# Two more output pairs by seven products, with the attention work visited inside them, in a retention and bilinear-FFN kernel on one Trainium2 core

## Chip, cores and metric

The kernel runs on one core of one Trainium2 chip. The metric is the device time of one execution in microseconds (us), the median of several runs. Engines are named as in the profile: PE (matrix products), DVE (VectorE), ACT (ScalarE), POOL (GpSimd), SP (it issues the transfers).

## The reference

A linear recurrent attention (retention) over 4 batches, 8 heads, 768 steps and 64 columns a head, whose output feeds a bilinear feed-forward layer over 3072 tokens:

```python
for t in range(S):
    state = gamma[None, :, None, None] * state + np.einsum('bhd,bhe->bhde', k[:, :, t], v[:, :, t])
    y[:, :, t] = scale * np.einsum('bhd,bhde->bhe', q[:, :, t], state)
...
x = np.ascontiguousarray(attn_out.transpose(0, 2, 1, 3)).reshape(B * S, H * D)
a = x @ w_a
b = x @ w_b
return (a * b @ w_out).astype(np.float32)
```

Inputs and output are float32. w_a and w_b are 512 x 1536, w_out is 1536 x 512.

## The kernel before

**Slots and tiles.** A slot is 128 tokens of one batch with all heads; there are 24. `TILES` groups them into eight tiles J of 4, 2, 2, 2, 2, 4, 4, 4 slots. J=0 holds slots 0 to 3, J=1 slots 4 and 5, J=2 slots 6 and 7, J=3 slots 8 and 9. The first six slots (three pairs) go through a chunked attention of their own (`casts2`, `flip2`, `scores2` and so on); the later ones go through `casts`, `turn` and `leave`.

**Attention of the later slots.** `casts(t)` scales k and q of slot t by decay tables into bf16 (`scaled`, POOL), has SP transpose them by DMA into `kqT`, casts v into `vb` (POOL), and after an odd slot has SP load the next two (`load_slot`: one transfer for k, two for q, one for v). `turn(new, old)` is PE's part for two slots at a time: it multiplies the older two with the running states (`inter`), makes the state products (`chunk_states`) and scores (`scores`) of the newer two, and finishes the older (`intra`). The sums of the state products run on DVE at once. Their casts to bf16 (`gst`, ACT) and the copies of a finished pair into the next tile's x (`leave`, ACT) are put into the list `later`, from which `catch_up(n)` takes n; the masking of the scores (DVE) is put into `unmasked`, from which `mask_now(n)` takes n.

**FFN of a tile.** For each of twelve blocks ft of 128 inner columns, `ffn_ab` makes a (4 matmuls, copied to SBUF as `asb` by ACT) and g (4 matmuls), and DVE multiplies g with `asb` into `ht` (line 625). The products' PSUM banks come from the pool `psff` with three banks; for the pairs in `SPARE` (tiles 2 to 4, odd ft) they come from the two banks of `psat` that are named y0 and y1. `parts` divides the matmuls of J=0 from ft 2 on into two halves of columns.

**Outputs.** J=0 and J=1 use `ffn_out`: for each slot 12 matmuls of 512 columns into one bank, which ACT copies out (line 659, 662). The tiles in `FAST` use `ffn_fast`, once for a pair of slots: a 2 x 2 block product by seven half-size products instead of eight, each of six matmuls of 256 columns (`product`, line 784). This needs sums of blocks of `ht` (`add` into `hsum`, four for each tile, line 682) and differences of blocks of w_out (`combine_o` into `wt_bf`, DVE, line 225). Between the products ACT takes snapshots of the banks (`keep`) and DVE adds banks and snapshots into the output (`plus`, line 799). A pair in `ASIDE` has the seventh product in a bank of its own, early; else it is the last one, added into R1.

**What sets the order.** The kernel writes every engine's order by hand: `seq` chains each instruction behind the one before it on its engine. Tile 1's twelve blocks (`blocks(1)`) stand ahead of J=0's outputs. The table `ahead` says what attention work is called at a visit: (J, ft) ahead of a block, (J, "o", i) ahead of output slot i, and "mid", "late" and "sums" inside `ffn_fast`. `adds_of` says after which ft the sums of a tile are made. Slots 8 and up have their k and q waiting in the raw buffers, 3 for each of k, q and v, which hold two slots each.

Of the kernel before, what the change touches and what calls it, by code (L numbers as in the profile page):

```python
# [9 lines left out]
F32 = mybir.dt.float32  # L10
# [17 lines left out]
def kernel(  # L28
# [209 lines left out]
    def scaled(eng, t, i):  # L238
        ktab, qtab = tabs[0] if t < 2 * PAIRS else tabs[1]
        dst, src, tab = kqb[t][:, i], raws["kq"[i], t], (ktab, qtab)[i][:, t % NCH]  # L240
        dst = dst.rearrange("p hp r d -> p r hp d")
        src = src.rearrange("p (r hp) d -> p r hp d", r=2)
        tab = tab.rearrange("p (r hp) o -> p r hp o", r=2).to_broadcast([P, 2, HP, D])
        if t < 10:
            seq(eng.tensor_tensor(dst, src, tab, op=ALU.mult))  # L245
        else:
            for r in range(2):
                seq(eng.tensor_tensor(dst[:, r], src[:, r], tab[:, r], op=ALU.mult))  # L248
# [6 lines left out]
    def casts(t, names="kqv"):  # L255
        if "k" in names:
            new_nat(t)
            scaled(nc.gpsimd, t, 0)
            scaled(nc.gpsimd, t, 1)
            kqT[t] = tra.tile([P, 2, HP, P], BF16, tag="kqT", name="kqT", bufs=6)  # L260
            seq(nc.sync.dma_start_transpose(
                out=kqT[t].rearrange("p a b c -> p (a b) c"),
                in_=kqb[t].rearrange("p a hp r d -> p (a hp r d)")))
# [326 lines left out]
    def parts(J, ft, c0, c1, n):  # L590
# [11 lines left out]
    def ffn_a(J, ft, c0=0, c1=None):  # L602
# [5 lines left out]
        for kt in range(KT):  # L608
            for b0, b1 in parts(J, ft, c0, c1, NFT):
                seq(nc.tensor.matmul(a[:, b0 - c0 : b1 - c0], wa_bf[:, kt, fs], xcols(J, kt, b0, b1),  # L610
                                     start=(kt == 0 and b0 == c0), stop=(kt == KT - 1 and b1 == c1),
                                     skip_group_check=True))
# [3 lines left out]
    def ffn_g(J, ft, c0=0, c1=None):  # L616
# [3 lines left out]
        for kt in range(KT):  # L620
            for b0, b1 in parts(J, ft, c0, c1, NFT):
# [45 lines left out]

    def rows(J, r, par, f0, f1):
        h = ht[J].rearrange("p (f r) (u par m) -> p r f u par m", r=2, par=2, m=P)
        return h[:, r, f0:f1, : TILES[J] // 2, par]  # L670
# [116 lines left out]
    def ffn_fast(J, u):  # L787
# [170 lines left out]
    for j in range(NO):  # L958
# [26 lines left out]
    def adds_of(J, ft):  # L985
        if J == 4:
# [34 lines left out]
    def blocks(J):  # L1021
        done = blocks_seven(J) if J in SEVEN else 0
        for ft in range(done, NFT):
# [3 lines left out]
            ffn_ab(J, ft)  # L1027
            if J in FAST:
# [52 lines left out]
```

## Time and profile before

| | us |
|---|---|
| median of 3 runs | 220.08 (219.37 to 220.78) |
| the profiled execution | 219.07 |
| its span, first to last instruction | 217.4 |
| PE busy in it | 210.2 (97%) |
| DVE busy | 143.5 (66%) |
| POOL busy | 120.1 (55%) |
| ACT busy | 96.9 (45%) |

The granted clock of TensorE was 1.000. A row of a timeline reads: start, duration (us), engine, line, operation, what is written and read, its shape, how many; in brackets the idle time ahead of it, and what ended that. A row of the chain has the same start, with what was on the path to the end. A group has its busy time in all, the mean of one in ns, and the idle time ahead of the group. The stage that the change touches lies between 40 and 70 us: tile 1's blocks from 40.08, the six output slots of J=0 and J=1 from 50.67 to 68.48, and from there on tile 2.

### The profile page before, as it was taken

How to read it: one execution, taken by the hardware profiler on the slowest of the kernel's cores; microseconds unless marked ns; L12 is line 12 of the kernel's file. 1: busy time of each engine (PE TensorE's matmuls, PEld its weight loads, DVE VectorE, ACT ScalarE, POOL GpSimd, SP SyncE). 2: the span in 40 equal slices, each digit the busy share in tenths (PEclk: the TensorE clock that was granted, in tenths of full speed). 3: DMA queues.
4: the chain of work that ended last, by engine and by line, in shares of the span. 5: the costliest groups of instructions: out<-in, count | busy, mean ns of one | idle time of the engine just before them, and what ended most of it. 6: DMA issues, size and time to landing. Idle time of an engine off the chain costs nothing.

```text
span 217.4 us, 7056 instructions
## 1 busy us (share of the span) xinstructions
PE 210.2 (97%) x2871; PEld 155.5 (72%) x2875; DVE 143.5 (66%) x324; ACT 96.9 (45%) x240; POOL 120.1 (55%) x185
## 2 busy tenths in 40 slices
PE   7799999999999999999999999999999999999993
PEld 6578898885446888888878445488665488666682
DVE  2784447647706787698785388987877674777731
ACT  3775244342426436437465342736441642444231
POOL 6557788684554625255462524646989508087400
PEclk9999999999999999999999999999999999999999
DMA  6999999988998998598878969997700002200022
GB/s 176 347 376 382 370 294 368 374 191 157 214 281 190 254 261 188 113 242 189 190 150 191 268 141 249 174 218 129 241 0 3 3 0 100 98 0 5 0 96 97
DMA packets 94832, 39.77 MB, mean 183 GB/s; under 512 B 76112, under 2 KB 91728, under 8 KB 94800
## 3 DMA queue, kind: packets, MB, share of 16 engines
q1 hardware_dynamic: 94656, 39.20, 69.1%
q8 instruction: 22, 0.36, 0.7%
q10 hardware_dynamic: 144, 0.13, 0.2%
q14 instruction: 10, 0.08, 0.1%
HBM read 28.31 MB, written 6.29 MB: 159 GB/s over the span
## 4 chain that ended last, share of the span: by engine, by line
PE 90%; DMA 3%; DVE 2%; POOL 1%; ACT 1%; issue 1%; SPq 0%; POOLq 0%; DVEq 0%
PE g L622 28%; PE a L610 22%; PE o L784 19%; PE o L659 7%; PE a L724 6%; DMA kf<-in_k_dram 3%; PE y L371 2%; PE at L326 1%; POOL kqb L245 1%; PE y L383 1%; PE st L296 1%; DVE ht L625 1%; PE tp L462 1%; PE st L503 1%; DVE aT L487 1%
## 5 line engine op out<-in xcount | busy, mean ns | idle before, releaser
L625 DVE TENSOR_TENSOR ht<-g,asb 128x256 bf16<-128x256 f32 (+1 forms) x98 | 53.8, 549 | 40.2 <-PE g L622 30.4
L622 PE MATMUL g<-xt,wb_bf 128*128 128x256 bf16 (+1 forms) x432 | 77.7, 308 | 0.3 <-ACT asb L614 0.3
L610 PE MATMUL a<-xt,wa_bf 128*128 128x256 bf16 (+1 forms) x368 | 60.9, 296 | 0.1
L614 ACT CAST asb<-a 128x256 bf16<-128x256 f32 (+1 forms) x82 | 36.9, 451 | 51.5 <-PE a L610 51.3
L622 PEld LDWEIGHTS <-wb_bf 128*128 128x128 bf16 x432 | 42.1, 98 | 16.5 <-issue 0.4
L610 PEld LDWEIGHTS <-wa_bf 128*128 128x128 bf16 x368 | 35.3, 98 | 12.3
L248 POOL TENSOR_TENSOR kqb<-kf,ktab 128x256 bf16<-128x256 f32 x28 | 17.2, 635 | 29.5 <-DMA kf<-in_k_dram 21.3
L209 POOL CAST vb<-vf 128x512 bf16<-128x512 f32 x24 | 14.7, 624 | 15.7 <-DMA vf<-in_v_dram 10.4
L784 PEld LDWEIGHTS <-hsum 128*128 128x128 bf16 x216 | 21.0, 98 | 2.7
L796 ACT COPY snap<-o 128x256 f32<-128x256 f32 x34 | 12.7, 375 | 19.6 <-PE o L784 19.4
L784 PE MATMUL o<-wt_bf,hsum 128*128 128x256 bf16 x162 | 19.4, 273 | 0.0
L248 POOL TENSOR_TENSOR kqb<-qf,qtab 128x256 bf16<-128x256 f32 x28 | 16.9, 625 | 3.0 <-DMA qf<-in_q_dram 3.0
L784 PEld LDWEIGHTS <-ht 128*128 128x128 bf16 x162 | 15.4, 98 | 2.5
L659 PE MATMUL o<-wo_bf,ht 128*128 128x512 bf16 x69 | 15.9, 379 | 0.2
L682 POOL TENSOR_TENSOR hsum<-ht 128x256 bf16<-128x256 bf16 (+1 forms) x15 | 11.0, 733 | 9.0 <-DVE ht L625 9.0
L310 DVE TENSOR_TENSOR sums<-st,sums 128x256 f32<-128x256 f32 x30 | 12.7, 423 | 1.5 <-PE st L296 0.2
L784 PE MATMUL o<-wo_bf,ht 128*128 128x256 bf16 x108 | 13.3, 273 | 0.0
L207 ACT CAST gst<-sums 128x256 bf16<-128x256 f32 x33 | 12.5, 412 | 0.5 <-DVE sums L308 0.3
L659 PEld LDWEIGHTS <-ht 128*128 128x128 bf16 x72 | 6.9, 98 | 7.9
L682 DVE TENSOR_TENSOR hsum<-ht 128x256 bf16<-128x256 bf16 (+1 forms) x32 | 12.1, 384 | 0.3
L245 POOL TENSOR_TENSOR kqb<-kf,ktab 128x512 bf16<-128x512 f32 x7 | 7.7, 1100 | 8.0 <-DMA kf<-in_k_dram 8.0
L332 DVE TENSOR_TENSOR aT<-at,mask 128x512 bf16<-128x512 f32 x18 | 12.1, 681 | 0.0
(101 smaller groups left out, 271.7 us busy)
## 6 DMA issues: line engine op xcount, KB each, us to landing
out_dram<-osb SPq DMA_DIRECT2D x11, 512.0 KB, 3.5
kf<-in_k_dram SPq DMA_DIRECT2D x18, 256.0 KB, 4.0
qf<-in_q_dram SPq DMA_DIRECT2D x36, 128.0 KB, 3.7
vf<-in_v_dram SPq DMA_DIRECT2D x18, 256.0 KB, 3.9
wsta<-in_moe_w_a_dram SPq DMA_DIRECT2D x6, 512.0 KB, 7.6
wstb<-in_moe_w_b_dram SPq DMA_DIRECT2D x6, 512.0 KB, 7.8
wsto<-in_moe_w_out_dram SPq DMA_DIRECT2D x6, 512.0 KB, 10.1
kf<-in_k_dram SPq DMA_DIRECT2D x3, 512.0 KB, 6.0
```

The source lines that it names most:

```text
L209: seq(engine.tensor_copy(dst, src))
L248: seq(eng.tensor_tensor(dst[:, r], src[:, r], tab[:, r], op=ALU.mult))
L310: seq(nc.vector.tensor_tensor(new, u[c][:, s], old, op=ALU.add))
L610: seq(nc.tensor.matmul(a[:, b0 - c0 : b1 - c0], wa_bf[:, kt, fs], xcols(J, kt, b0, b1), start=(kt == 0 and b0 == c0), stop=(kt == KT - 1 a ...
L614: seq(nc.scalar.copy(asb, a))
L622: seq(nc.tensor.matmul(g[:, b0 - c0 : b1 - c0], wb_bf[:, kt, fs], xcols(J, kt, b0, b1), start=(kt == 0 and b0 == c0), stop=(kt == KT - 1 a ...
L625: seq(nc.vector.tensor_tensor(ht[J][:, ft, c0:c1], g, asbs.pop((J, ft, c0)), op=ALU.mult))
L659: seq(nc.tensor.matmul(o, ht[J][:, ft, i * P : (i + 1) * P], wo_bf[:, f, 2 * r : 2 * r + 2, :].rearrange("p a d -> p (a d)"), start=(ft == ...
L682: seq(eng.tensor_tensor(s[which], x(), y(), op=op))
L724: seq(nc.tensor.matmul(R, w, x, start=(first and k == 0), stop=(k == 1), skip_group_check=True))
L784: seq(nc.tensor.matmul(R[:, :DH], lhs, (wo_bf, wt_bf)[w][:, f, m, :], start=(first and f == 0), stop=(f == NH - 1), skip_group_check=True))
L796: seq(nc.scalar.copy(snap[:, i], R[:, :DH]))
```

## The change

J=1 joins `FAST` and `ASIDE`. J=0's slots 0 and 1 keep `ffn_out`; slots 2 and 3 become one call `ffn_fast(0, 1)`, and J=1's two slots one call `ffn_fast(1, 0)`. Both share one set of `hsum` tiles. J=0's sums (all six block pairs at once, 768 columns) are made by DVE behind tile 1's blocks 2 to 5, J=1's first four block pairs (512 columns) behind its blocks 8 to 11, and the last two (256 columns) ahead of `ffn_fast(0, 1)`.

The turns are visited inside: `turn(6, None)` at "mid" of J=0's pair, `turn(8, 6)` at "sums" of J=1's. Slot 8's k and q are loaded ahead of slot 6's transpose, slot 8 is scaled one output slot earlier, slots 6 to 9 are scaled in two halves, the v casts of slots 8 and 9 run on ACT at a new visit "last", and those of 10 and 11 on POOL behind k and q of 11. J=0's blocks 8 to 11 aren't divided into column halves any more.

```diff
-FAST = (2, 3, 4, 5, 6, 7)
-ASIDE = ((2, 0), (3, 0), (4, 0), (5, 0), (6, 0), (6, 1), (7, 0))
+FAST = (1, 2, 3, 4, 5, 6, 7)
+ASIDE = ((1, 0), (2, 0), (3, 0), (4, 0), (5, 0), (6, 0), (6, 1), (7, 0))
@@ scaled
-        if t < 10:
+        if t < 2 * PAIRS:
             seq(eng.tensor_tensor(dst, src, tab, op=ALU.mult))
@@ casts
-    def casts(t, names="kqv"):
+    def casts(t, names="kqv", eng=nc.gpsimd):
...
+            if t == 6:
+                load_slot(8, "kq")
             seq(nc.sync.dma_start_transpose(
...
-                    load_slot(t + 1, names)
+                    if (t, names) != (7, "kq"):
+                        load_slot(t + 1, names)
                     load_slot(t + 2, names)
         if "v" in names:
-            cast(nc.gpsimd, vb[t], raws["v", t])
+            cast(eng, vb[t], raws["v", t])
@@ parts
-        if J == 0 and 2 <= ft < n:
+        if J == 0 and 2 <= ft < 8:
@@ rows, add
+    def fast_pairs(J):
+        return slice(1, 2) if J == 0 else slice(0, TILES[J] // 2)
...
+        if J == 1:
+            hsum[1] = hsum[0]
...
-        s = [x[:, f0:f1, : TILES[J] // 2] for x in hsum[J]]
+        s = [x[:, f0:f1, fast_pairs(J)] for x in hsum[J]]
@@ ffn_fast
-        R5 = bank()
+        R5 = psat.tile([P, DM], F32, tag="y0", name="o") if J == 0 else bank()
         product(R5, J, u, ("s", 0), (1, 0), True)
         keep(3, R5)
+        visit(J, "last", u)
@@ ahead
-        (0, "o", 2): [(turn, 6, None), (casts, 8, "kq")],
-        (0, "o", 3): [(casts, 9, "kq"), (casts, 8, "v"), (casts, 9, "v")],
-        (1, "o", 1): [(turn, 8, 6, D_), (casts, 10)],
-        (2, 2): [(casts, 11)], (2, 7): [(casts, 12)], (2, "o", 0): [(turn, 10, 8), (casts, 13)],
+        (0, "o", 1): [(casts, 8, "kq")], (0, "o", 2): [(casts, 9, "kq")] + [(add, 1, i, 4, 6) for i in range(4)],
+        (0, "mid"): [(turn, 6, None)], (0, "last", 1): [(casts, 8, "v", A_), (casts, 9, "v", A_)],
+        (1, "sums", 0): [(turn, 8, 6), (casts, 10, "kq"), (catch_up, 1)],
+        (2, 2): [(casts, 11, "kq"), (casts, 10, "v"), (casts, 11, "v")], (2, 7): [(casts, 12)],
+        (2, "o", 0): [(turn, 10, 8), (casts, 13)],
@@ adds_of, blocks, the loop over outputs
+        if J == 1:
+            return {ft: [(ft - 8, 0, 4)] for ft in range(8, 12)}.get(ft, ())
...
+            if J == 1 and 2 <= ft < 6:
+                add(0, ft - 2, 0, NH)
...
-            if J not in FAST:
+            if J == 0 and i == 2:
+                ffn_fast(0, 1)
+            elif J == 0 and i < 2:
                 ffn_out(J, i)
```

DVE's queue during tile 1's blocks, before: the last products of J=0, the twelve of tile 1 (`ht<-g,asb` of 128x256), then the differences of w_out.

```order
L625 TENSOR_TENSOR ht<-g,asb 128x512
L209 CAST xt<-y 128x8x64
L625 TENSOR_TENSOR ht<-g,asb 128x512
L625 TENSOR_TENSOR ht<-g,asb 128x256 x12
L225 TENSOR_TENSOR wt_bf<-wo_bf 128x3x256
```

The same place now, from tile 1's first products on (`hsum` are the sums):

```order
L628 TENSOR_TENSOR ht<-g,asb 128x256 x3
L690 TENSOR_TENSOR hsum<-ht 128x6x128
L628 TENSOR_TENSOR ht<-g,asb 128x256
L690 TENSOR_TENSOR hsum<-hsum,ht 128x6x128
L628 TENSOR_TENSOR ht<-g,asb 128x256
L690 TENSOR_TENSOR hsum<-ht 128x6x128
L628 TENSOR_TENSOR ht<-g,asb 128x256
L690 TENSOR_TENSOR hsum<-ht,hsum 128x6x128
L628 TENSOR_TENSOR ht<-g,asb 128x256 x3
L690 TENSOR_TENSOR hsum<-ht 128x4x128
L628 TENSOR_TENSOR ht<-g,asb 128x256
L690 TENSOR_TENSOR hsum<-hsum,ht 128x4x128
```

Sums of J=0 and of J=1 now stand between tile 1's products, which stood together.

DVE's queue around the outputs, before: the last difference of w_out, the sums of slot 6's and 7's state products (`sums<-st`), the masks (`aT<-at`), the same for slots 8 and 9, and tile 2's first products.

```order
L225 TENSOR_TENSOR wt_bf<-wo_bf,wt_bf 128x3x256
L308 COPY sums<-st 128x256
L310 TENSOR_TENSOR sums<-st,sums 128x256 x3
L332 TENSOR_TENSOR aT<-at,mask 128x512 x2
L348 COPY mark<-bq 128x1
L310 TENSOR_TENSOR sums<-st,sums 128x256 x4
```

The same place now, up to the end of J=0's pair (`osb<-o,snap` are the output sums):

```order
L225 TENSOR_TENSOR wt_bf<-wo_bf,wt_bf 128x3x256
L690 TENSOR_TENSOR hsum<-ht 128x2x128
L690 TENSOR_TENSOR hsum<-hsum,ht 128x2x128
L690 TENSOR_TENSOR hsum<-ht 128x2x128
L690 TENSOR_TENSOR hsum<-ht,hsum 128x2x128
L311 COPY sums<-st 128x256
L313 TENSOR_TENSOR sums<-st,sums 128x256 x3
L807 TENSOR_TENSOR osb<-o,snap 128x256
L335 TENSOR_TENSOR aT<-at,mask 128x512
L807 TENSOR_TENSOR osb<-o,snap 128x256
L335 TENSOR_TENSOR aT<-at,mask 128x512
L807 TENSOR_TENSOR osb<-o,snap 128x256 x2
```

Four sums now stand ahead of the state sums, and output sums between the masks.

SP's queue from slot 7's loads to slot 9's, before (k, q in two transfers, v; the transposes write `kqT`):

```order
L103 DMA vf<-in_v_dram 128x8x64
L261 DMA_TRANSPOSE kqT<-kqb 128x8x128 x2
L103 DMA kf<-in_k_dram 128x8x64
L101 DMA qf<-in_q_dram 64x8x64 x2
L103 DMA kf<-in_k_dram 128x8x64
L101 DMA qf<-in_q_dram 64x8x64 x2
L103 DMA vf<-in_v_dram 128x8x64 x2
```

And now:

```order
L103 DMA vf<-in_v_dram 128x8x64
L103 DMA kf<-in_k_dram 128x8x64
L101 DMA qf<-in_q_dram 64x8x64 x2
L263 DMA_TRANSPOSE kqT<-kqb 128x8x128 x2
L103 DMA kf<-in_k_dram 128x8x64
L101 DMA qf<-in_q_dram 64x8x64 x2
L103 DMA vf<-in_v_dram 128x8x64 x2
```

Slot 8's k and q went ahead of the transposes of slots 6 and 7; slot 9's stayed behind them.

More of the change, by code (lines that the diff above doesn't have):

```diff
@@ L588, with parts @@
     asbs = {}
-    def parts(J, ft, c0, c1, n):
-        if J == 0 and 2 <= ft < n:
+    def parts(J, ft, c0, c1):
+        if J == 0 and 2 <= ft < 8:
             return [(c0, (c0 + c1) // 2), ((c0 + c1) // 2, c1)]
@@ L608, in ffn_a @@
         for kt in range(KT):
-            for b0, b1 in parts(J, ft, c0, c1, NFT):
+            for b0, b1 in parts(J, ft, c0, c1):
                 seq(nc.tensor.matmul(a[:, b0 - c0 : b1 - c0], wa_bf[:, kt, fs], xcols(J, kt, b0, b1),
@@ L620, in ffn_g @@
         for kt in range(KT):
-            for b0, b1 in parts(J, ft, c0, c1, NFT):
+            for b0, b1 in parts(J, ft, c0, c1):
                 seq(nc.tensor.matmul(g[:, b0 - c0 : b1 - c0], wb_bf[:, kt, fs], xcols(J, kt, b0, b1),
@@ L666 @@
     hsum = {}
+    def fast_pairs(J):
+        return slice(1, 2) if J == 0 else slice(0, TILES[J] // 2)
     def rows(J, r, par, f0, f1):
         h = ht[J].rearrange("p (f r) (u par m) -> p r f u par m", r=2, par=2, m=P)
-        return h[:, r, f0:f1, : TILES[J] // 2, par]
+        return h[:, r, f0:f1, fast_pairs(J), par]
     def add(J, which, f0, f1, eng=nc.vector):
+        if J == 1:
+            hsum[1] = hsum[0]
         if J not in hsum:
             hsum[J] = [wstage.tile([P, NH, 2, P], BF16, tag="w" + "ab"[i % 2], name="hsum") for i in range(4)]
-        s = [x[:, f0:f1, : TILES[J] // 2] for x in hsum[J]]
+        s = [x[:, f0:f1, fast_pairs(J)] for x in hsum[J]]
         x, y, op = {
```

## The prediction

> **What bounds the kernel now.** I read the page's chain first, then PE's timeline from 50 to 85 us, where the changed outputs lie, then DVE's and POOL's timelines beside it.
>
> ```profile
> PE 90%; DMA 3%; DVE 2%; POOL 1%; ACT 1%; issue 1%; SPq 0%; POOLq 0%; DVEq 0%
> ```
>
> The chain that ends last is PE for 90% of the span. So work taken from PE is time saved, provided PE then waits for nobody. PE's timeline of the stage:
>
> ```profile
> 50.67 5.34 PE L659 MATMUL o<-wo_bf,ht 128*128 128x512 bf16 x23
> 55.95 0.45 PE L296 MATMUL st<-vb,kqb 64*64 64x64 bf16 x32
> ...
> 56.64 7.94 PE L659 MATMUL o<-wo_bf,ht 128*128 128x512 bf16 x35
> 64.51 0.28 PE L371 MATMUL y<-kqT,gst 64*64 64x64 bf16 x10
> ...
> 65.88 2.76 PE L659 MATMUL o<-wo_bf,ht 128*128 128x512 bf16 x11
> 68.48 0.60 PE L610 MATMUL a<-xt,wa_bf 128*128 128x256 bf16 x4
> ...
> 80.24 1.48 PE L784 MATMUL o<-wo_bf,ht 128*128 128x256 bf16 x12
> ...
> 84.84 0.60 PE L610 MATMUL a<-xt,wa_bf 128*128 128x256 bf16 x4
> ```
>
> Six output products of twelve matmuls (three records are missing) run from 50.67 to 68.48 with two turns between, and PE has no gap there. A turn is the attention work of two slots: 0.69 us at 55.95, 1.37 us at 64.51. After 68.48 PE is the chain to the end, so a shift there stays.
>
> **The saving on PE.** The six outputs take 5.28, 7.87 and 2.60 us, 15.75 in all, or 5.25 a pair. Seven products of six matmuls, as J=2 has them, run from 80.24 to 84.84: 4.60, or 0.66 each. Two pairs: 2 x 0.65 = 1.30 us less. The undivided matmuls of the first tile's ft 8 to 11 are priced here:
>
> ```profile
> 26.48 1.75 PE a L610 x16
> ...
> 119.50 0.86 PE a L610 x4
> ```
>
> Sixteen halves 1.75, eight whole ones 2 x 0.86: 0.03 for two groups, 0.1 us for the eight groups. Together -1.4 us.
>
> **What DVE gets, and when.** DVE has 4 adds of 128x768 behind J=1's ft 2 to 5, 4 of 128x512 behind ft 8 to 11, and 4 of 128x256 between the two plain outputs and the first seven products; before it had none of them. PE and DVE in J=1:
>
> ```profile
> 41.07 0.60 PE L610 MATMUL a<-xt,wa_bf 128*128 128x256 bf16 x4
> ...
> 41.94 0.60 PE L610 MATMUL a<-xt,wa_bf 128*128 128x256 bf16 x4
> ```
> ```profile
> 41.23 0.42 DVE L625 TENSOR_TENSOR ht<-g,asb 128x256 bf16<-128x256 f32 x1 [0.22 <-PE g L622]
> ...
> 51.29 0.58 DVE L225 TENSOR_TENSOR wt_bf<-wo_bf 128x768 bf16<-128x768 bf16 x1
> ...
> 54.85 0.55 DVE L225 TENSOR_TENSOR wt_bf<-wo_bf,wt_bf 128x768 bf16<-128x768 bf16 x1
> ...
> 56.47 0.42 DVE L308 COPY sums<-st 128x256 f32<-128x256 f32 x1 [1.06 <-PE st L296]
> 56.99 1.34 DVE L310 TENSOR_TENSOR sums<-st,sums 128x256 f32<-128x256 f32 x3
> ```
>
> One ft is 0.87 us of PE (41.07 to 41.94) and 0.42 of DVE. J=1 uses three banks in turn, so the a of ft 2 (41.94) takes the bank that the ht of ft 0 frees at 41.65: DVE may be late by 0.29 us, and beyond that PE stands. An add of 768 columns is as wide as the L225 row, 0.55 alone. So 4 x (0.42 + 0.55 - 0.87) = 0.40 us of lateness, if DVE has SBUF to itself. It hasn't. POOL works without a break there, and rows of J=2 show what an add costs beside it:
>
> ```profile
> 72.70 0.29 DVE L682 TENSOR_TENSOR hsum<-ht 128x256 bf16<-128x256 bf16 x1
> 73.45 0.73 DVE L682 TENSOR_TENSOR hsum<-hsum,ht 128x256 bf16<-128x256 bf16 x1
> 74.44 0.36 DVE L682 TENSOR_TENSOR hsum<-ht 128x256 bf16<-128x256 bf16 x1
> 75.20 0.28 DVE L682 TENSOR_TENSOR hsum<-ht,hsum 128x256 bf16<-128x256 bf16 x1
> ...
> 80.92 0.55 DVE L682 TENSOR_TENSOR hsum<-ht 128x256 bf16<-128x256 bf16 x1
> 81.50 0.64 DVE L682 TENSOR_TENSOR hsum<-hsum,ht 128x256 bf16<-128x256 bf16 x1
> 82.40 0.36 DVE L682 TENSOR_TENSOR hsum<-ht 128x256 bf16<-128x256 bf16 x1
> 82.69 0.28 DVE L682 TENSOR_TENSOR hsum<-ht,hsum 128x256 bf16<-128x256 bf16 x1
> ```
> ```profile
> 44.72 1.04 POOL L209 CAST wo_bf<-wsto 128x1024 bf16<-128x1024 f32 x1 [0.79 <-DMA wsto<-in_moe_w_out_dram]
> 45.72 1.04 POOL L245 TENSOR_TENSOR kqb<-kf,ktab 128x512 bf16<-128x512 f32 x1
> ...
> 50.85 0.61 POOL L209 CAST vb<-vf 128x512 bf16<-128x512 f32 x1
> 55.57 1.04 POOL L245 TENSOR_TENSOR kqb<-kf,ktab 128x512 bf16<-128x512 f32 x1 [4.11 <-DMA kf<-in_k_dram]
> ...
> 72.75 1.28 POOL L248 TENSOR_TENSOR kqb<-kf,ktab 128x256 bf16<-128x256 f32 x2
> ...
> 81.38 1.23 POOL L248 TENSOR_TENSOR kqb<-qf,qtab 128x256 bf16<-128x256 f32 x2
> ```
>
> Beside POOL's 0.6 us halves eight adds took 0.28 to 0.73 us; over the 0.28 of one alone that is 1.25 us for eight, 0.16 each, 0.45 at worst. In J=1 POOL casts the output weights (1.04) and scales slots 6 and 7. Bounds of the wait of one add: 0 and 1.04, a whole cast; I take 0.16, the mean of the nearest rows. Then ft 2 to 5 are late by 0.40 + 0.64 = 1.04, less the 0.29 of room: PE stands 0.8 us. For ft 8 to 11:
>
> ```profile
> L682 DVE TENSOR_TENSOR hsum<-ht 128x512 bf16<-128x512 bf16 x5 | 2.3, 463 | 0.0
> ```
>
> 0.42 + 0.46 + 0.16 - 0.87 = 0.17, three times ahead of a product, less 0.29: 0.2 us. J=1 costs PE 1.0 us, so its outputs begin at 50.67 - 0.1 + 1.0 = 51.6.
>
> The Trainium skill, page "SBUF — State Buffer", section "Who interferes with whom", has it that a VectorE instruction with two inputs in SBUF and a GpSimd one that reads SBUF exclude each other, and that the later one blocks until the earlier has finished. The 0.73 against 0.28 agrees. By this rule an add that comes as a cast starts pays the cast's whole 1.04, and the sum would lie with the second rival below.
>
> **The wait in the first seven products.** Before, DVE combined the weights from 51.29 to 55.40 (8 ops, 4.1 us) while POOL stood idle for slot 8's k (the 4.11 at 55.57), and was then idle 1.06 us until the turn's state products. Now k and q of slot 8 are loaded ahead of two transposes, and POOL fills that idle time with them. DVE comes to the combining late: 51.29 - 0.1 + 1.0, 0.3 of used-up room and 0.6 for the last add, 53.1. Eight ops with 0.16 of wait each end at 58.5, four adds of 0.28 + 0.16 at 60.3. PE has its plain outputs behind it at 51.6 + 5.25 = 56.8, two products at 58.1, the state products at 58.6. So DVE is 1.7 us late for the copy and three adds of sums (0.42 and 1.34). Behind these are queued, on ACT, a snapshot; on DVE, an output sum, a mask, another output sum:
>
> ```profile
> L796 ACT COPY snap<-o 128x256 f32<-128x256 f32 x34 | 12.7, 375 | 19.6 <-PE o L784 19.4
> L207 ACT CAST gst<-sums 128x256 bf16<-128x256 f32 x33 | 12.5, 412 | 0.5 <-DVE sums L308 0.3
> ```
> ```profile
> 85.06 0.68 DVE L332 TENSOR_TENSOR aT<-at,mask 128x512 bf16<-128x512 f32 x1
> 85.66 0.41 DVE L799 TENSOR_TENSOR osb<-o,snap 128x256 f32<-128x256 f32 x1
> ```
>
> ACT: first sum at 60.7, its cast 0.41, the snapshot of R1 0.38: 61.5. Only then may PE add the fifth product into R1; it was ready at 58.1 + 0.69 (turn) + 1.3 (two products) = 60.1. 1.4 us of standing. Products five and six end at 62.8. The seventh again needs R1, after DVE's sums (62.1), output sum, mask and output sum (0.41 + 0.68 + 0.41): 63.6, another 0.8 us. Pair: 2.2 us. With DVE on time the second of these waits is still 0.5 us, since its queue (1.8 + 0.4 + 0.7 + 0.4 = 3.3 us from the state products) is longer than PE's (a quarter us of scores and four products, 2.9).
>
> J=1's pair: its products and the turn inside it meet no such queue, since the masks of slots 6 and 7 are done by 64.7 and the turn is visited behind four of seven products. PE: 63.6 + 0.7 + four products 2.6 + turn 1.4 + three products 2.0 = 70.3 against 68.48.
>
> **Edits priced at nothing.** Scaling slots 6 to 9 in halves lengthens POOL by eight times 0.2 us (1.28 for two against 1.04), slots 6 and 7 by 0.8; covered as long as slot 9's transpose is in time. That chain:
>
> ```profile
> 61.18 1.59 SPq L261 DMA_TRANSPOSE kqT<-kqb  x1
> ```
> ```profile
> kqT<-kqb SPq DMA_TRANSPOSE x18, 3.9
> ```
> ```profile
> 65.01 0.49 PE L326 MATMUL at<-kqT 64*64 64x64 bf16 x32
> ```
>
> Issued at 61.18 with 3.9 to landing, its reader at 65.01 had next to no slack. POOL, busy without a break to about 60, would let it go at about 61.3, to land at 65.2; the reader now stands inside J=1's pair at about 67.5. Two us of room. The v casts of slots 8 and 9 move from POOL to ACT (1.2 us, as 50.85 shows one on POOL), behind the last snapshot, where ACT waits for PE anyway. Stores of the first pair go behind six more loads on SP; nobody waits for them, since a buffer of the other pair is free.
>
> **The sum.** -1.4 + 1.0 + 2.2 = +1.8 us. The profiled execution took 219.07 (span 217.4, 1.67 around it), so 220.9. The median of the runs shown, 220.08, is 1.0 above that execution: 221.8 as a median.
>
> **Rivals.** First, not slower: the adds fall between POOL's instructions, as 72.70 and 75.20 did (0.29, 0.28). Then J=1 costs 0.40 - 0.29 = 0.1, the pair its own 0.5: -0.8, 219.3 as a median. From there the sum grows by 4 + 13 times the mean wait of the 20 adds and combinations, the 13 once DVE has used up its 0.3 us of lead, so it decides where that wait is below about 0.07 us. Against it speaks that POOL's idle 4.11 is gone. Chance 0.24.
>
> Second, dearer: each of the 20 waits 0.25, the mean of the five rows that did wait (0.45, 0.27, 0.36 and twice 0.08). J=1 then costs 0.4 + 1.0 - 0.3 and 0.5, and the pair 12 x 0.09 + 0.1 more, 3.4: +3.6 us, 223.7. For it: POOL has no pause between its instructions there, and its casts are longer than the halves. Against it: three of the eight rows show nothing. Chance 0.16.
>
> Third, slot 9's transpose lands behind its reader: POOL pays for DVE's locks too. It needs 2 us more delay, and would add 1 to 2 us: 223.3. Chance 0.08.
>
> **Chances and range.** My forecast, +0.8 to +2.8 (220.9 to 222.9): 0.52. About 1%, 2.2 us, is what a measurement of this kernel can tell from no change, so slower means above 222.3. A quarter of the forecast lies there, with nearly all of the second and third rival: 0.36. Faster (under 217.9) needs all of the 1.4 and more from elsewhere: 0.04. The rest, 0.60, is within 1%. Eight in ten from the first rival's middle to the second's: 218.9 to 223.8.
>
> **What would show it.** Right: DVE's hsum rows of 128x768 between 43 and 48 us at over 0.6, PE waiting for ht in J=1, outputs starting after 51.3, sums copied over 1 us after the state products, J=2's first a near 70. Wrong: those adds at 0.55, POOL idle while DVE combines, J=2's first a before 68, or a PE wait for a transpose.

## The result and the profile after

| | before | after |
|---|---|---|
| median, us (8 runs each, taken together) | 220.37 (219.37 to 222.63) | 222.14 (221.41 to 223.13) |
| profiled execution, us | 219.07 | 223.13 |
| its span, us | 217.4 | 221.4 |
| tile 1, its first a to the first output, us | 10.60 | 11.67 |
| outputs, the first one to tile 2's first a, us | 17.80 | 20.75 |
| from there to the last matmul, us | 145.13 | 145.26 |

The ratio of the times is 1.010, with a 95% interval of 1.0076 to 1.0125: slower by about one per cent. Ratios, here and below, leave out executions that took over 1.5% more than the fastest of the same kernel: one of twelve of "second pair alone" and four of twelve of the last kernel of the table below, three of the kernel before. The profiled execution after is the slowest of its eight. Its extra 4.06 us lie in tile 1 (1.07) and in the outputs (2.95); behind tile 2's first a next to nothing changed (0.13).

The page after, the chain's shares by engine and the clock's row of the 40 slices:

```profile
PEclk9999999999979999999999999999999999999999
...
PE 80%; DVE 8%; DMA 7%; POOL 1%; issue 1%; ACT 1%; SPq 0%; DVEq 0%; POOLq 0%
```

DVE is now 8% of the chain that ends last, where it had 2%, and one slice shows a lower granted clock. PE's timeline of the stage (start, duration, what; in brackets the idle time ahead and who ended it):

```profile
46.39 0.60 PE L613 MATMUL a<-xt,wa_bf 128*128 128x256 bf16 x4 [0.65 <-DVE ht L628]
...
51.66 5.34 PE L662 MATMUL o<-wo_bf,ht 128*128 128x512 bf16 x24
...
58.24 0.45 PE L299 MATMUL st<-vb,kqb 64*64 64x64 bf16 x32
...
62.51 0.82 PE L792 MATMUL o<-wt_bf,hsum 128*128 128x256 bf16 x6 [2.10 <-ACT snap L804]
...
64.51 1.44 PE L792 MATMUL o<-wt_bf,ht 128*128 128x256 bf16 x6 [0.49 <-DVE osb L807]
65.75 2.21 PE L792 MATMUL o<-wo_bf,ht 128*128 128x256 bf16 x12
...
72.41 0.60 PE L613 MATMUL a<-xt,wa_bf 128*128 128x256 bf16 x4
```

PE, which had no gap here before, stands once in tile 1 behind DVE's `ht`, 2.10 us ahead of the first pair's fifth product behind ACT's snapshot, and 0.49 ahead of the seventh behind DVE's output sum. Behind the long stand, the products at 64.51 and 65.75 take 1.44 and 2.21 us, where six and twelve such matmuls take 0.82 and 1.47 elsewhere: 1.36 us lost. The table of windows (length, PE busy, PEld, DVE, ACT, POOL, granted clock, DMA share, GB/s) shows why:

```profile
62.00:64.00 2.00, 1.49 (x12) 1.17 (x12) 1.93 (x5) 2.00 (x7) 0.00 (x0) 0.96 0.55 110
64.00:66.00 2.00, 1.50 (x9) 1.05 (x8) 1.39 (x4) 0.70 (x4) 0.60 (x2) 0.50 1.04 234
66.00:68.00 2.00, 2.00 (x14) 1.55 (x13) 0.00 (x0) 0.73 (x2) 1.90 (x5) 0.69 1.10 248
```

The granted clock of TensorE is 0.50 in the second of these stretches and partly so in the other two. Ahead of all this, DVE's timeline of the same kernel:

```profile
44.58 1.43 DVE L690 TENSOR_TENSOR hsum<-hsum,ht 128x768 bf16<-128x768 bf16 x1
...
46.81 0.41 DVE L628 TENSOR_TENSOR ht<-g,asb 128x256 bf16<-128x256 f32 x1
47.15 0.63 DVE L690 TENSOR_TENSOR hsum<-ht,hsum 128x768 bf16<-128x768 bf16 x1
47.70 0.41 DVE L628 TENSOR_TENSOR ht<-g,asb 128x256 bf16<-128x256 f32 x1
...
53.03 0.96 DVE L225 TENSOR_TENSOR wt_bf<-wo_bf 128x768 bf16<-128x768 bf16 x1
...
57.93 0.96 DVE L225 TENSOR_TENSOR wt_bf<-wo_bf 128x768 bf16<-128x768 bf16 x1
58.82 0.96 DVE L225 TENSOR_TENSOR wt_bf<-wo_bf,wt_bf 128x768 bf16<-128x768 bf16 x1
59.70 0.69 DVE L690 TENSOR_TENSOR hsum<-ht 128x256 bf16<-128x256 bf16 x1
...
61.34 0.41 DVE L311 COPY sums<-st 128x256 f32<-128x256 f32 x1
```

and POOL's and ACT's:

```profile
44.56 1.04 POOL L209 CAST wo_bf<-wsto 128x1024 bf16<-128x1024 f32 x1 [0.64 <-DMA wsto<-in_moe_w_out_dram]
...
58.44 1.81 POOL L248 TENSOR_TENSOR kqb<-qf,qtab 128x256 bf16<-128x256 f32 x2
...
65.40 1.18 POOL L248 TENSOR_TENSOR kqb<-kf,ktab 128x256 bf16<-128x256 f32 x2 [4.54 <-DMA kf<-in_k_dram]
```
```profile
61.79 0.40 ACT L207 CAST gst<-sums 128x256 bf16<-128x256 f32 x1 [3.68 <-DVE sums L311]
62.10 0.36 ACT L804 COPY snap<-o 128x256 f32<-128x256 f32 x1
```

Read from the bottom up, this is a queue. PE waits for ACT's snapshot of R1 (62.10), which stands behind the cast of the state, which waits 3.68 us for DVE's state sums (61.34), which stand behind the sums of `ht` and eight combining adds (53.03 to 59.70). The state products that the sums read had ended at 58.7 on PE (58.24 and 0.45). DVE has no gap from 53.03 to the state sums; the queue is long because its eight adds are, and because four sums (59.70 to 61.34) have joined it.

The groups by line show how long, tile 1 and the outputs taken together, after and then before (busy, mean ns of one):

```profile
L225 DVE TENSOR_TENSOR wt_bf<-wo_bf,wt_bf 128x768 bf16<-128x768 bf16 x4 | 3.6, 906 | 0.1
L225 DVE TENSOR_TENSOR wt_bf<-wo_bf 128x768 bf16<-128x768 bf16 x4 | 3.4, 858 | 0.0
```
```profile
L225 DVE TENSOR_TENSOR wt_bf<-wo_bf 128x768 bf16<-128x768 bf16 x4 | 2.2, 560 | 0.0
L225 DVE TENSOR_TENSOR wt_bf<-wo_bf,wt_bf 128x768 bf16<-128x768 bf16 x4 | 2.2, 554 | 0.1
```

The same eight adds cost 0.88 in place of 0.56 us each: 0.33 of wait for one, counted from the 0.55 of most single rows before.

### The profile page after: what moved, and what is told of

It is laid out like the page before. It is cut to its first block, busy times and chain, and to the rows that moved or that the text cites. A ratio compares the mean times of both kernels' runs of the same rounds, so it can differ in the third digit from the quotient of the medians.

```text
span 221.4 us, 7098 instructions
## 1 busy us (share of the span) xinstructions
PE 212.0 (96%) x2879; PEld 156.9 (71%) x2879; DVE 154.3 (70%) x341; ACT 98.0 (44%) x247; POOL 124.2 (56%) x192
## 4 chain that ended last, share of the span: by engine, by line
PE 80%; DVE 8%; DMA 7%; POOL 1%; issue 1%; ACT 1%; SPq 0%; DVEq 0%; POOLq 0%
PE g L625 25%; PE o L792 22%; PE a L613 20%; PE a L732 5%; DMA qf<-in_q_dram 4%; DVE wt_bf L225 3%; DMA kf<-in_k_dram 3%; DVE hsum L690 2%; PE y L374 2%; POOL kqb L245 1%; PE y L386 1%; PE at L329 1%; DVE ht L628 1%; PE st L299 1%; PE tp L465 1%
## 5 line engine op out<-in xcount | busy, mean ns | idle before, releaser
L248 POOL TENSOR_TENSOR kqb<-kf,ktab 128x256 bf16<-128x256 f32 x36 | 23.8, 680 | 35.9 <-DMA kf<-in_k_dram 23.6
L792 PEld LDWEIGHTS <-hsum 128*128 128x128 bf16 x264 | 25.5, 98 | 5.7 <-issue 2.3
L792 PE MATMUL o<-wt_bf,hsum 128*128 128x256 bf16 x198 | 24.1, 273 | 2.1 <-ACT snap L804 2.1
L248 POOL TENSOR_TENSOR kqb<-qf,qtab 128x256 bf16<-128x256 f32 x36 | 23.8, 681 | 2.4 <-DMA qf<-in_q_dram 2.3
L792 PEld LDWEIGHTS <-ht 128*128 128x128 bf16 x198 | 19.6, 101 | 4.5 <-issue 0.7
L792 PE MATMUL o<-wo_bf,ht 128*128 128x256 bf16 x132 | 17.0, 281 | 0.0
L807 DVE TENSOR_TENSOR osb<-o,snap 128x256 f32<-128x256 f32 x25 | 10.5, 418 | 7.8 <-PE o L792 5.9
L690 DVE TENSOR_TENSOR hsum<-ht 128x256 bf16<-128x256 bf16 (+2 forms) x38 | 14.9, 396 | 0.3
L842 DVE TENSOR_TENSOR osb<-o,snap 128x512 f32<-128x512 f32 x8 | 5.5, 692 | 8.7 <-PE o L792 7.2
L710 POOL TENSOR_TENSOR ta<-wa_bf 128x256 bf16<-128x256 bf16 x10 | 7.1, 706 | 7.5 <-DVE osb L807 7.5
```

What stands on the lines that cost most here:

```text
L690: seq(eng.tensor_tensor(s[which], x(), y(), op=op))
L792: seq(nc.tensor.matmul(R[:, :DH], lhs, (wo_bf, wt_bf)[w][:, f, m, :], start=(first and f == 0), stop=(f == NH - 1), skip_group_check=True))
```

## The experiments

All ratios are to the kernel before, run on the same chip beside it, where it had medians of 219.5 to 219.7. "Outputs" is the time from the first output to tile 2's first a, read off PE's timeline; without any stand it should be 17.80 - 1.30 = 16.5.

| kernel | ratio (95%) | tile 1 | outputs |
|---|---|---|---|
| the changed kernel again | 1.0106 (1.0072 to 1.0141) | 10.84 | 19.55 |
| POOL only writes | 0.9978 (0.9958 to 0.9998) | 10.81 | 16.87 |
| second pair's last sums later | 1.0006 (0.9986 to 1.0025) | 10.84 | 17.80 |
| first pair's sums later | 1.0110 (1.0076 to 1.0144) | 10.63 | 19.32 |
| the stand filled | 1.0125 (1.0098 to 1.0152) | 10.58 | 19.05 |
| second pair alone | 1.0028 (1.0014 to 1.0043) | 10.58 | 18.59 |
| first pair alone | 1.0005 (0.9992 to 1.0017) | 10.84 | 17.59 |
| loads not ahead | 1.0089 (1.0056 to 1.0123) | 10.84 | 18.87 |
| sums spread | 0.9963 (0.9932 to 0.9994) | 10.65 | 18.30 |
| and masks later | 0.9959 (0.9931 to 0.9988) | 10.66 | 18.02 |
| and one cast of v less | 0.9946 (0.9932 to 0.9959) | 10.65 | 16.72 |
| the same, loads not ahead | 1.0018 (0.9992 to 1.0044) | 10.83 | 16.58 |

**The changed kernel again.** No edit.

> The changed kernel once more, unaltered, beside the kernels of this call. The profile before it showed a stand of 1.07 us in tile 1, 2.3 and 0.7 us in J=0's pair, and half the clock for 3.4 us behind these. Theory (POOL and DVE wait for each other's reads): the pair's stands are there again within 0.3 us, since DVE's queue has no slack there; the stand in tile 1 is anywhere from 0 to 1.2, by whether a sum comes ahead of a cast of w_out or behind it. Rival (the stands are chance): the pair's stands differ by more than 1 us. The clock: below 1.000 in most runs if the stand causes the drop. Time 221.4 to 222.6.

Median 221.68. In its profile the clock stays at 1.00, and the same two stands are there on PE:

```profile
62.22 0.81 PE L792 MATMUL o<-wt_bf,hsum 128*128 128x256 bf16 x6 [2.21 <-ACT snap L804]
...
64.21 0.81 PE L792 MATMUL o<-wt_bf,ht 128*128 128x256 bf16 x6 [0.53 <-DVE osb L807]
```

Tile 1 costs only 0.24 more than before here. The outputs' excess over 16.5 is 3.05, of which the rows give 2.21 + 0.53; of the other 0.31, some 0.2 is there without any stand too (16.72 in the best kernel below). So the pair's stand is the rule; the 1.07 of tile 1 isn't, and the half clock comes and goes: the mean clock was clearly lower (0.990 and 0.992) in two of these six executions, where most were expected to show it.

**POOL only writes.** Is it POOL's reading of SBUF that makes DVE's adds long? This kernel leaves out POOL's scaling of slots 6 to 9 and its casts of v of slots 6 and 7, and fills the buffers with a constant.

```diff
-            scaled(nc.gpsimd, t, 0)
-            scaled(nc.gpsimd, t, 1)
+            if t < 10:
+                for i in range(2):
+                    seq(nc.gpsimd.memset(kqb[t][:, i], 0.01))
+            else:
+                scaled(nc.gpsimd, t, 0)
+                scaled(nc.gpsimd, t, 1)
...
-            cast(eng, vb[t], raws["v", t])
+            if t < 8:
+                seq(nc.gpsimd.memset(vb[t], 0.01))
+            else:
+                cast(eng, vb[t], raws["v", t])
```

> This kernel leaves out the scaling of k and q of slots 6 to 9 and the v casts of slots 6 and 7: POOL fills those buffers with a constant instead, which reads nothing from SBUF. DVE's instructions are the same as in the changed kernel. Theory (POOL and DVE wait for each other's reads of SBUF): of the 768-column sums the third and fourth, and all eight differences of w_out, take 0.55 us each as they do alone (0.63 and 0.55 to 0.96 in the changed kernel), the state sums of slots 6 and 7 start within 0.5 us of their products' end, PE's stand ahead of the fifth product (2.1) goes below 0.3, and the time is 219.3 to 220.3. Rival (DVE simply has too much work between 43 and 65 us, whatever POOL does): the stands remain at over 1.5 us and the time stays near 222.

Median 219.02, a little better than expected. DVE's groups and its timeline in this kernel:

```profile
L225 DVE TENSOR_TENSOR wt_bf<-wo_bf,wt_bf 128x768 bf16<-128x768 bf16 x4 | 2.2, 554 | 0.1
L225 DVE TENSOR_TENSOR wt_bf<-wo_bf 128x768 bf16<-128x768 bf16 x4 | 2.2, 550 | 0.0
```
```profile
58.28 0.43 DVE L318 COPY sums<-st 128x256 f32<-128x256 f32 x1 [1.15 <-PE st L306]
```

All eight adds are at 0.55 again, DVE waits 1.15 us for the state products instead of coming late, and both long stands are gone. The one add of tile 1 that stayed long, 0.98, still met the cast of w_out. But this kernel doesn't settle the question for the eight adds, since POOL had nothing to do beside them. POOL's timeline, and the second of two sums of DVE's in tile 1 that lie beside fills:

```profile
46.49 0.99 POOL L260 MEMSET kqb<- 128x512 bf16 x2
...
47.89 1.92 POOL L260 MEMSET kqb<- 128x512 bf16 x4
61.08 0.61 POOL L209 CAST vb<-vf 128x512 bf16<-128x512 f32 x1 [11.27 <-DMA vf<-in_v_dram]
```
```profile
46.62 0.54 DVE L697 TENSOR_TENSOR hsum<-ht,hsum 128x768 bf16<-128x768 bf16 x1
```

The fills, which wait for no load, had ended at 49.81, and the eight adds ran from 52.13 to 56.2. So for them the kernel shows what they cost with POOL idle. What writing alone does is shown by the two sums at 45.82 and 46.62: 0.54 each beside fills, 0.63 each beside scalings in the changed kernel (46.26 and 47.15).

**The second pair's last sums behind the first pair's products.** Four short adds leave the queue ahead of the state sums.

```diff
-        (0, "o", 1): [(casts, 8, "kq")], (0, "o", 2): [(casts, 9, "kq")] + [(add, 1, i, 4, 6) for i in range(4)],
+        (0, "o", 1): [(casts, 8, "kq")], (0, "o", 2): [(casts, 9, "kq")],
+        (1, "o", 0): [(add, 1, i, 4, 6) for i in range(4)],
```

> The four 256-column sums of tile 1 move from ahead of J=0's pair to behind it. Theory (PE's stand ahead of the fifth product is DVE's lateness, and these four stand in the queue): the state sums start 1.6 us earlier, the stand of 2.1 falls to about 0.5, the stand ahead of the seventh product stays near 0.5, the clock stays at 1.000, and the time is 219.6 to 220.8. Rival (the stand has another cause, such as the transpose or the loads of slots 8 and 9, or the v casts on ACT): the stand stays at 2 us and the time near 222.

Median 219.88, as expected. On DVE the state sums begin 1.65 us sooner than in the profile after, and on PE the fifth product's stand falls about as much:

```profile
59.69 0.41 DVE L311 COPY sums<-st 128x256 f32<-128x256 f32 x1
```
```profile
60.86 0.81 PE L792 MATMUL o<-wt_bf,hsum 128*128 128x256 bf16 x6 [0.46 <-ACT snap L804]
```

**The first pair's sums two blocks later**, clear of w_out's casts.

```diff
-            if J == 1 and 2 <= ft < 6:
-                add(0, ft - 2, 0, NH)
+            if J == 1 and 4 <= ft < 8:
+                add(0, ft - 4, 0, NH)
```

> J=0's four 768-column sums stand behind tile 1's blocks 4 to 7 instead of 2 to 5, past POOL's two last casts of w_out (1.04 us each). Theory (the waits are for the POOL instruction in progress): each of them takes 0.6 to 0.8 us, tile 1's stand falls from 1.0 to about 0.4 us, the time is 221.2 to 221.8. Rival (the sums' own work makes the stand): it stays at 1.0 and the time at 222.1.

Median 221.75. Tile 1 doesn't stand any more (10.63), yet the time is that of the changed kernel. PE's fifth product in this kernel:

```profile
61.70 0.82 PE L792 MATMUL o<-wt_bf,hsum 128*128 128x256 bf16 x6 [1.97 <-ACT snap L804]
```

Its stand is still 1.97 us, and the outputs take 19.32 us, as in the repeated run (19.55). What is won ahead of a late queue is waited for at its end.

**The stand filled** with 18 idle matmuls ahead of the fifth product, to keep PE busy.

```diff
+FILL = 18
...
         keep(3, R5)
+        if J == 0:
+            warm(FILL, psat, "y1")
         visit(J, "last", u)
```

> 18 idle matmuls of 256 columns (0.109 us each, 2.0 in all) into a free bank stand ahead of the fifth product, where PE stood 2.1 us. Nothing else changes. Theory of the clock (PE's stand lets its granted clock fall to half for 3.4 us, which showed from 63.5 to 66.9 us): the clock stays at 1.000, the products behind the stand take 0.66 us each again, and the time falls by 0.8 to 1.5 us, to 220.6 to 221.3. Rival (the clock fell for another reason, or costs nothing because DVE is late anyway): the time stays at 222.1 or rises by what the fill is too long.

Median 222.38: a miss. The clock was 0.998 to 1.000 in all six runs, so the half clock stayed away, but the time didn't fall. PE's timeline shows the filling at 59.19, and stands of another kind in tile 6, which the repeated run of the changed kernel doesn't have:

```profile
59.19 2.13 PE L587 MATMUL idle<-zero 128*128 128x256 bf16 x18
...
150.87 1.05 PE L793 MATMUL o<-wo_bf,ht 128*128 128x256 bf16 x8 [0.38 <-issue]
```

From tile 2's first a to the last matmul it took 146.36 us, against 145.17 in that run. The rows of stands there give 0.6 of these 1.19 us (0.38 at 150.87 and 0.2 at 146.38, behind a sum of DVE's). What PE waited for at 150.87 ("issue": nothing that the profile shows) wasn't tried, nor whether the filling brought it.

**One pair at a time.** The second pair alone by seven products, the first one plain:

```diff
-        if J == 1:
-            hsum[1] = hsum[0]
...
-        (0, "o", 1): [(casts, 8, "kq")], (0, "o", 2): [(casts, 9, "kq")] + [(add, 1, i, 4, 6) for i in range(4)],
-        (0, "mid"): [(turn, 6, None)], (0, "last", 1): [(casts, 8, "v", A_), (casts, 9, "v", A_)],
+        (0, "o", 1): [(casts, 8, "kq")], (0, "o", 2): [(casts, 9, "kq")] + [(add, 1, i, 4, 6) for i in range(4)] + [(turn, 6, None)],
+        (0, "o", 3): [(casts, 8, "v", A_), (casts, 9, "v", A_)],
...
-            if J == 1 and 2 <= ft < 6:
-                add(0, ft - 2, 0, NH)
...
-            if J == 0 and i == 2:
-                ffn_fast(0, 1)
-            elif J == 0 and i < 2:
+            if J == 0:
```

> Only J=1's pair goes by seven products; J=0 keeps its four plain outputs, and its 768-column sums fall away; turn(6) stands ahead of output slot 2, the v casts of slots 8 and 9 ahead of slot 3. Theory (the cost is DVE's lateness in J=0's pair): PE doesn't wait for DVE's state sums between plain outputs, no stand over 0.5 us, saving 0.65 for one pair: 219.0 to 219.8 against 219.6 to 220.4 before. Rival (the visits inside a pair or the loads ahead cost the time): 220.5 or more.

Median 220.17, above the expected range by 0.4. PE and ACT in this kernel:

```profile
64.28 0.82 PE L790 MATMUL o<-wt_bf,ht 128*128 128x256 bf16 x6 [0.71 <-ACT osb L665]
```
```profile
60.37 1.85 ACT L207 CAST gst<-sums 128x256 bf16<-128x256 f32 x4 [3.83 <-DVE sums L311]
...
62.60 1.14 ACT L207 CAST vb<-vf 128x512 bf16<-128x512 f32 x2
63.64 0.58 ACT L665 COPY osb<-o 128x512 f32<-128x512 f32 x1
```

ACT waits 3.83 us for DVE's late sums, and its copies of the plain outputs, which free PE's banks, stand behind it and behind the casts of v. The same queue reaches PE by another door. The stands of PE that its profile shows, 0.71 and one of 0.21, don't make up the whole excess: its outputs take 18.59 us, where one pair by seven products should make it 17.15.

The first pair alone:

```diff
-FAST = (1, 2, 3, 4, 5, 6, 7)
-ASIDE = ((1, 0), (2, 0), (3, 0), (4, 0), (5, 0), (6, 0), (6, 1), (7, 0))
+FAST = (2, 3, 4, 5, 6, 7)
+ASIDE = ((2, 0), (3, 0), (4, 0), (5, 0), (6, 0), (6, 1), (7, 0))
...
-        (0, "o", 1): [(casts, 8, "kq")], (0, "o", 2): [(casts, 9, "kq")] + [(add, 1, i, 4, 6) for i in range(4)],
+        (0, "o", 1): [(casts, 8, "kq")], (0, "o", 2): [(casts, 9, "kq")],
-        (1, "sums", 0): [(turn, 8, 6), (casts, 10, "kq"), (catch_up, 1)],
+        (1, "o", 1): [(turn, 8, 6, D_), (casts, 10, "kq")],
...
-            elif J == 0 and i < 2:
+            elif J == 1 or (J == 0 and i < 2):
```

> Only J=0's pair goes by seven products; J=1 keeps its two plain outputs with turn(8, 6) between them, and its sums fall away. Theory (DVE late by the waits of eight differences of w_out, 6.7 instead of 4.1 us, then the queue ahead of the fifth and seventh product): stands of about 0.6 to 1.0 and 0.7 us in the pair, 219.9 to 221.0. Rival (the four 256-column sums alone make the stand): no stand, 219.0 to 219.5.

Median 219.73, slightly below the expected range and nearer to the rival: of the expected stands only 0.21 us ahead of the seventh product came. The second pair's sums no longer stand between tile 1's products or ahead of the state sums, so DVE reaches these at 57.97 although six of the eight adds are still long.

**Slot 8's k and q loaded behind the transposes again.**

```diff
-            if t == 6:
-                load_slot(8, "kq")
...
-                    if (t, names) != (7, "kq"):
-                        load_slot(t + 1, names)
+                    load_slot(t + 1, names)
```

> Slot 8's k and q are loaded behind the transposes of slots 6 and 7 again, as before; the rest of the change stays. Theory (POOL's work on slot 8 fills the time in which DVE combines w_out, and each difference waits for it): at least five of the eight differences take 0.55 to 0.6 us, DVE reaches the state sums 1 us or more earlier, and the stand ahead of the fifth product falls to 1.3 us or less; but slot 9's transpose comes later, and if its reader now waits, what was gained is lost again there. Time 220.8 to 222.0. Rival (the loads ahead are what keeps POOL from being late, and the lock matters little): stands unchanged, plus a wait for the transpose, above 222.5.

Median 221.18. With POOL idle for want of slot 8 the eight adds take 0.55 each, and the state sums begin at 58.86, 2.2 us sooner than in the repeated run (61.04). But PE then stands ahead of the second pair, for a reason that POOL, ACT and PE show in turn:

```profile
63.35 0.61 POOL L209 CAST vb<-vf 128x512 bf16<-128x512 f32 x1 [1.58 <-DMA vf<-in_v_dram]
```
```profile
63.99 0.62 ACT L207 CAST vb<-vf 128x512 bf16<-128x512 f32 x1 [0.96 <-POOL vb L209]
```
```profile
65.54 0.81 PE L789 MATMUL o<-wt_bf,ht 128*128 128x256 bf16 x6 [1.38 <-ACT osb L855]
```

v comes later with the later loads, POOL casts it later, ACT waits for POOL, and behind that cast stands the copy that frees the second pair's bank. Part of the gain on DVE is given back there.

**The sums spread.** The loads ahead stay; the sums get out of the way of what PE waits for.

```diff
-        (0, "o", 1): [(casts, 8, "kq")], (0, "o", 2): [(casts, 9, "kq")] + [(add, 1, i, 4, 6) for i in range(4)],
+        (0, "o", 1): [(casts, 8, "kq")], (0, "o", 2): [(casts, 9, "kq")],
+        (1, "o", 0): [(add, 1, i, 0, NH) for i in range(4)],
...
-            return {ft: [(ft - 8, 0, 4)] for ft in range(8, 12)}.get(ft, ())
+            return ()
...
-            if J == 1 and 2 <= ft < 6:
-                add(0, ft - 2, 0, NH)
+            if J == 1 and ft in (4, 6, 8, 10):
+                add(0, ft // 2 - 2, 0, NH)
```

> The computation is that of the changed kernel; only the places of sums on DVE move: the first pair's four sums of 768 columns stand behind tile 1's blocks 4, 6, 8 and 10 instead of 2 to 5, and all of the second pair's sums behind the first pair's products. Queue theory (DVE reaches the eight combining adds and the state sums late because 768-column adds that share their time with POOL are packed ahead of them): the products of tile 1 no longer stand (0 to 0.3 us in place of 0.24 to 1.07), the state sums begin at 59.0 to 59.7 (61.0 to 61.3 in the changed kernel), the stand ahead of the fifth product falls from 2.1-2.4 to 0.3-0.6 us, the one of 0.69 ahead of the seventh stays; 219.0 to 219.9 us against 219.5 of the kernel before, ratio 0.998 to 1.002. Rival, that the seven products in themselves (weights switched more often, visits inside the pair) are what costs: 221 us or more, ratio above 1.006, with the stands gone.

Median 219.02, at the lower end. The state sums begin at 57.76, when their products end, and the fifth product doesn't stand, which speaks against the rival. The stand of 0.5 ahead of the seventh has shrunk to 0.22. A new one of 1.27 us lies ahead of the second pair, the one that the run with later loads had shown.

**And the first pair's inner mask later**, so that the output sum stands ahead of it.

```diff
-        mask_now(1)
+        if J:
+            mask_now(1)
```

> As the run before it, and in the first pair the mask of the visit inside it is left to the end of the pair, so that the output sum which frees the buffer of the seventh product stands first on DVE. If the 0.69 us ahead of the seventh product is DVE's mask (0.68 us) standing before that sum, this stand goes and the products end 0.5 to 0.7 us earlier: 218.5 to 219.4 us, ratio 0.995 to 0.999. If the stand is ACT's copy of the first part coming late behind the state's casts, it stays and the time equals that of the run before within 0.2 us.

Median 218.98. The seventh product follows without a stand, but the time is that of the run before within 0.1 us: PE waits a little later for ACT instead. PE and ACT:

```profile
60.64 0.81 PE L792 MATMUL o<-wt_bf,ht 128*128 128x256 bf16 x6
...
63.92 0.82 PE L792 MATMUL o<-wt_bf,ht 128*128 128x256 bf16 x6 [1.15 <-ACT osb L859]
```
```profile
62.37 0.62 ACT L207 CAST vb<-vf 128x512 bf16<-128x512 f32 x1 [2.04 <-POOL vb L209]
```

The cast at 62.37 waits for POOL's cast into the same tile. In `casts` the loop over the loads uses the name `names` again, and leaves it as "v". So `casts(9, "kq")` casts slot 9's v too, on POOL, and the change's `casts(9, "v", A_)` writes the same values once more on ACT. The kernel before does it twice as well, both times on POOL; what leaving one out would be worth there wasn't run.

**That second cast left out.**

```diff
-        (0, "last", 1): [(casts, 8, "v", A_), (casts, 9, "v", A_)],
+        (0, "last", 1): [(casts, 8, "v", A_)],
```

> The spread sums and the later mask of the run before it, less ACT's cast of slot 9's v: the same values are cast by POOL already, with slot 9's k and q, so ACT's is a second writing of the same tile, which waits 2.0 us for POOL's. Queue theory on ACT (the plain-output copy that frees the buffer of the second pair's first product stands behind that cast): the stand of 1.15 us ahead of that product falls to 0.0-0.4 us, the products of both pairs end 0.8-1.1 us earlier and the time is 217.8 to 218.6 us against 219.6 of the kernel before, ratio 0.990 to 0.995. Rival, that the copy is late for another reason (its own product, the state's casts): the stand stays within 0.3 us of 1.15 and the ratio at 0.996.

Median 218.53 against 219.68: as expected. PE has no stand left between tile 1 and tile 2:

```profile
61.38 1.47 PE L792 MATMUL o<-wo_bf,ht 128*128 128x256 bf16 x12
62.69 0.82 PE L792 MATMUL o<-wt_bf,ht 128*128 128x256 bf16 x6
```

Its outputs take 16.72 us, its tile 1 10.65. It is the fastest of all, 0.5% below the kernel before and 1.6% below the changed one (0.9946 to 1.0106). Its eight combining adds still take 0.88 us each; nobody waits for them. The 0.5% is not the change's alone, since the kernel before still has its second cast.

**The same, with the loads not ahead.**

```diff
-            if t == 6:
-                load_slot(8, "kq")
...
-                    if (t, names) != (7, "kq"):
-                        load_slot(t + 1, names)
+                    load_slot(t + 1, names)
```

> The run before it, with slot 8's k and q loaded behind slot 6's transposes again, so that POOL works beside fewer of DVE's eight combining adds. Queue theory on DVE: the state's sums already begin when their products end there, so the shorter adds (0.55 in place of 0.85-0.96 us, some 2 us in all) buy nothing, while slot 8's and 9's v come later and may hold the state's casts: the time is that of the run before it, or up to 1 us more. Rival, that the length of the adds beside POOL counts in itself: 0.5 to 2 us less than the run before it.

Median 220.16 of the executions that the ratio counts, 0.7% above the run before it: in the expected direction and more than expected. All but one of the adds take 0.55 us, and that buys nothing. Instead a transpose further on comes late, as PE shows:

```profile
80.05 0.32 PE L326 MATMUL at<-kqT 64*64 64x64 bf16 x16 [0.73 <-DMA kqT<-kqb]
```

That stand explains about half of the some 1.6 us. In the profiled execution another 0.56 lies ahead of tile 1 (its first a at 40.64 against 40.08), where the profiled executions of all these kernels differ by up to 0.8; where the rest lies in the other runs stays open.

## Why the prediction was right where it was, and where it wasn't

The predicted time, 221.8, lies 0.3 from the median, and the forecast of +1.8 us beside 1.77 measured (222.14 - 220.37). The ratio came out on the edge of 1%. That it came out so near is partly luck: two of its terms were off in opposite directions. In the repeated run, tile 1 cost 0.24 in place of 1.0, and the outputs 3.05 above what they take without stands in place of 2.2.

**The saving on PE, -1.4.** Right. With nothing else in the way the outputs take 16.72 in place of 17.80 us, 1.1 of the 1.3. The 0.1 for the undivided matmuls can't be told apart.

**Tile 1, +1.0.** The mechanism was right, and the term as high as predicted in the profiled execution alone (1.07). In the repeated run, and in four others with the sums at the same place, it was 0.2, in a fifth nothing. "I take 0.16, the mean of the nearest rows" spread the wait over all adds. What it came to hung mostly on a single add: the one at 44.58 came 0.02 us behind a cast of w_out and took 1.43, a wait of 0.88; in the repeated run the same add took 0.98. The term's other part, "4 x (0.42 + 0.55 - 0.87)", was too high too: it adds durations, and DVE's rows overlap. The product at 46.81, the add of 0.63 at 47.15 and the next product at 47.70 start within 0.89 us, where 0.41 and 0.63 make 1.04, so that such a block makes DVE hardly later than PE's 0.87. The four sums of 512 columns cost PE nothing.

**The first pair, +2.2.** Undersized. The step that failed is "Eight ops with 0.16 of wait each end at 58.5". They ended at 59.70, with 0.33 of wait each; the state sums began at 61.34 and not at 60.3; the fifth product stood 2.10 to 2.21 and not 1.4; the seventh 0.5, not 0.8. The eight rows that the 0.16 came from take in three that met no wait, and one of these had POOL idle beside it: the sum at 82.69, behind POOL's two that end at 82.61 (81.38 and 1.23). The eight adds stand in a row beside a POOL that is also busy in a row. There the two take turns, and seven of the eight adds wait. The second rival's 0.25, from the rows that did wait, was nearer.

**The path of the wait** was right: DVE's adds, the state sums, ACT's cast, the snapshot, the fifth product. Leaving out POOL's work beside the adds removed the stand, and moving other sums out of that queue, with the adds still long, took it from 2.1 to 0.46 or away. So the length of the adds matters only through the lateness of the queue behind them. The rule of the Trainium skill, page "SBUF — State Buffer", section "Who interferes with whom", that only a GpSimd instruction that reads SBUF holds up a DVE one with two inputs there, agrees with the two sums that lie beside POOL's fills (0.54 against 0.63 beside scalings); the eight adds don't bear on it, since they had an idle POOL beside them there.

**The first rival** (not slower, -0.8) is about what one gets where the adds have POOL idle beside them: 0.9978, about -0.5 us. **The third**, slot 9's transpose late, didn't happen. SP and the reader on PE, in the kernel after:

```profile
56.92 5.14 SPq L263 DMA_TRANSPOSE kqT<-kqb  x2
```
```profile
69.59 0.49 PE L329 MATMUL at<-kqT 64*64 64x64 bf16 x32
```

The transposes of slots 8 and 9 were issued by 62.06, and the reader at 69.59 had no wait ahead of it. The room was there.

**Edits priced at nothing.** ACT's casts of v were indeed hidden, but by DVE's lateness. With that gone they became a stand of 1.2 us, and half of them wasn't needed at all: slot 9's v hadn't moved to ACT, it was cast on both. That the loads ahead are worth something by themselves wasn't in the sum; with the queue on time they are worth 0.7% by the ratios, of which the profiles account for about half.

**The clock** wasn't in the prediction. It made 1.4 us of the profiled execution's 4.06, which is why that one is dearer than the sum. Four of the eight executions behind the median had a mean clock of 0.990 to 0.992.

## What to carry to other kernels

Price a wait between two engines from rows in which both are busy without a break, as they will be; the mean of rows of which some had nobody beside them came out at half (0.16 for 0.33). When an add becomes longer, ask first whether the instruction behind it on its queue is already late: moving four short adds out of the way was worth 2.2 us (1.0106 to 1.0006), taking POOL's work from beside the long ones 2.8 (to 0.9978). And behind a stand that is removed, the next one stands ready: here it was a cast that only the first had hidden, and leaving it out brought the version that beats both.

## What the runs showed of the hardware

Two engines that hold each other up don't simply follow one another. A POOL instruction on two inputs alone takes 0.59 us (1.18 for two), an add of 768 columns 0.55, or 0.51 in a row of eight before (4.1 us). Had each waited for the whole of the other, a round of both would take 1.1. It takes 0.89 (DVE's adds at 57.93 and 58.82, POOL's two in 1.81); both records grow longer, to 0.9 or more each, so that a wait shows as a long record and not as idle time.

A stand of PE of some 2 us may bring half clock behind it. The three kernels with such a stand (the changed kernel, its repetition, and the one with the first sums later) ran 20 times: in 9 the mean granted clock was 0.990 to 0.992, with a median of 222.6 us, in the other 11 it was 0.997 to 1.000, with 221.4. In the other ten kernels, whose longest stand in a profile is 1.4 us, four of all 99 executions showed 0.992 or less, and no other less than 0.996; in the kernel before, which has no stand there, it was three of the 86 beside these. The Trainium skill, page "TensorE: Matmul & The Clock Gate", speaks of an idle window of about 3.4 us ahead of half clock; in the profile after, half clock set in 1.3 us behind the end of a stand of 2.1 us (the 0.96 over 62 to 64 us puts its start at 63.8), and that stand is shorter. How much of the median this makes isn't settled, since the run in which the stand was filled kept its clock and lost the time elsewhere.
